# Attention and feed-forward in one Trainium2 kernel: loading, casting and turning the first five half batches by units of tokens, feed-forward chunks of 384, and a new order of work

## The chip, the cores and the metric

The kernel runs on one core of one Trainium2 chip. The metric is the device time of one execution in microseconds (us). The kernel before takes 337.58 us in the median of the four runs taken beside the changed one (337.21 to 337.86). Two kernels are compared only on fast runs of the same chip, unless the text says otherwise.

## The reference, cut to what matters

```python
# q, k, v: (batch 8, heads 8, sequence 576, head_dim 64), float32
scores = q @ k^T / 8
rel = i - j
mask  = (0 <= rel < 32)                        for heads 0..3   # plain window
mask  = (0 <= rel < 128) & (rel % 4 == 0)      for heads 4..7   # dilated window
attn  = softmax(where(mask, scores, -1e9))
x     = (attn @ v) as (4608 tokens, 512)       # heads side by side
h     = x @ w_in                               # (4608, 2048)
out   = max(0.01 h, h) @ w_out                 # (4608, 512), float32
```

## The kernel before: the parts that matter here

The work is a hand-written list of steps, and every engine does its part of the steps in the order of the list. A half batch `n` is four heads of one batch: even `n` has the plain window, odd `n` the dilated one. `lq`, `lv`, `lw` load q and k, v, and weights. `cq`, `cv`, `cw` cast them to float16 on VectorE (`V`), GpSimd (`P`) or ScalarE (`A`). `B` turns q and k on TensorE, `T` turns them by a DMA. `S`, `M`, `D` are scores, mask and values of one attention unit (three units to a half batch). `I:c:j` is a tile of the first feed-forward layer for chunk `c` of tokens, `O:t:g` a quarter of the second layer's tile `t`. `Z` is filler: matmuls on zeros whose result nobody reads.

```python
CHUNKS = [(0, 384), (384, 192), (576, 448)] + [(1024 + 512 * i, 512) for i in range(7)]
NPE = 5                     # the first five half batches are turned on TensorE

def load_qk(n, pairs=(0, 1)):
    b, kind = divmod(n, 2)
    base = (b * H + 4 * kind) * S * D
    for nm, x in (("q", q), ("k", k)):
        ...
        if n >= NPE:
            nc.sync.dma_start(t[0:96], rows_ap(x, base, [[D, 96], [96 * D, 24], [1, D]]))
        elif len(pairs) == 2:
            nc.sync.dma_start(t[:, 0:18, :].rearrange("p (a t) d -> p a (t d)", a=2),
                              rows_ap(x, base, [[9 * D, 128], [2 * S * D, 2], [1, 9 * D]]))
        else:                # one pair of heads: 128 partitions of 9 tokens
            p = pairs[0]
            nc.sync.dma_start(t[:, 9 * p:9 * p + 9, :].rearrange("p t d -> p (t d)"),
                              rows_ap(x, base + 2 * S * D * p, [[9 * D, 128], [1, 9 * D]]))
...
def pe_transpose(n, p, nm, eng):      # 9 x 2 transposes of 64 x 64 for one pair, then one copy
    ...
def values(u, log_recip=False, pool=None):
    ...
    if log_recip:                     # 1 / den on ScalarE
        nc.scalar.activation(out=ln, in_=den[:, 0:384], func=AF.Ln)
        nc.scalar.activation(out=rec, in_=ln, func=AF.Exp, scale=-1.0)
    else:                             # 1 / den on VectorE
        nc.vector.reciprocal(out=rec, in_=den[:, 0:384])
...
def ff_in(c, j):
    t0, w = CHUNKS[c]
    hp = psm.tile([128, 512], FP32, tag="pm", name="hp")
    for i in range(4):
        nc.tensor.matmul(hp[:, 0:w], w1[j // 4][:, i, j % 4::4], xT[:, i, x0:x0 + w], ...)
    nc.scalar.activation(out=gt[:, j, g0:g0 + w], in_=hp[:, 0:w], func=AF.Prelu, alpha=0.01)
```

The softmax here doesn't subtract the row's maximum and nothing guards it: scores larger than these inputs give would overflow.

## Time and profile before

| | kernel before |
|---|---|
| time | 337.58 us |
| TensorE busy | 97% |
| first feed-forward matmul | 27.40 us |
| first matmul of chunk 2 | 63.68 us |
| filler | 59 matmuls, 21.8 us |

Each digit of the page's slices is a fortieth of the span (8.4 us here), in tenths: the TensorE clock that was granted, and the mean busy share of the 16 DMA engines.

```profile
PEclk9999999999999999999999999999999999999999
DMA  6999899790499399999669945700110020011011
```

The clock row shows full speed throughout, but it can't be trusted for the first 7 us: there the fillers of a pair start 380 to 400 ns apart, and from 8.3 us on 215. The DMA engines are nearly full from the second slice on. (Shares a little above 1 occur in the views by stretch; read them as full.) The second view is the first line of the timeline of SyncE, the engine that issues the loads; its columns are start, duration, and the transfer issued.

```profile
0.80 0.41 SPq L149 DMA_DIRECT2D qf<-in_q_dram  x1
```

### The profile page before, as it was taken

To read this page: it belongs to the slowest core of one execution; us is meant where nothing else is said; L and a number is where in the kernel's file an instruction comes from. 1 tells how busy PE (TensorE), PEld (TensorE's weight loads), DVE (VectorE), ACT (ScalarE), POOL (GpSimd) and SP (SyncE) were. 2 spreads that over 40 slices of the span, in tenths; PEclk is the share of its full clock that TensorE was granted. 3 is DMA by queue.
4 is the path that set the end of the run, shared out by engine and by line. 5 is a ranking of instruction groups with operands and counts; after the bars stand their busy time and mean duration, and the time that the engine had idled before them with its cause. 6 is when DMAs were issued, how large, how long until landed. Compare 5 with 4: busy or idle time off the path is not lost.

```text
span 337.6 us, 6297 instructions
## 1 busy us (share of the span) xinstructions
PE 326.7 (97%) x2639; PEld 168.6 (50%) x2639; DVE 173.0 (51%) x190; ACT 171.3 (51%) x293; POOL 95.0 (28%) x93
## 2 busy tenths in 40 slices
PE   7999898999999899999999999999999999999995
PEld 1456576554544455445545544554455445445542
DVE  6354598631416958777786687677677200000000
ACT  2388788762434763356426743565255416524611
POOL 5446674434004335547071533300000000000000
PEclk9999999999999999999999999999999999999999
DMA  6999899790499399999669945700110020011011
GB/s 208 287 392 376 285 292 337 177 193 31 135 261 283 86 234 242 227 288 222 155 166 242 212 107 162 174 3 0 64 62 2 8 85 33 0 62 64 0 57 67
DMA packets 111243, 53.02 MB, mean 157 GB/s; under 512 B 96880, under 2 KB 101488, under 8 KB 110704
## 3 DMA queue, kind: packets, MB, share of 16 engines
q1 hardware_dynamic: 106032, 43.20, 51.5%
q10 hardware_dynamic: 5184, 9.44, 7.7%
q8 instruction: 20, 0.33, 0.4%
q14 instruction: 7, 0.06, 0.1%
HBM read 36.70 MB, written 9.44 MB: 137 GB/s over the span
## 4 chain that ended last, share of the span: by engine, by line
PE 90%; DVE 5%; issue 1%; DMA 1%; ACT 1%; DVEq 0%
PE op L353 36%; PE hp L343 34%; PE wp L396 6%; PE sps L255 6%; PE den L281 4%; PE o L289 2%; PE tp L206 2%; DVE rec L297 2%; DVE em L265 2%; DMA out_dram<-ob 1%; DVE xT L313 1%; PE sps L243 1%; ACT ln L294 0%; ACT ob L357 0%; DVE vh L189 0%
## 5 line engine op out<-in xcount | busy, mean ns | idle before, releaser
L343 PE MATMUL hp<-xT,w 128*128 128x512 f16 (+3 forms) x640 | 130.9, 359 | 0.0
L353 PE MATMUL op<-w,gt 128*128 128x512 f16 x576 | 128.8, 379 | 0.0
L345 ACT ACTIVATE gt<-hp 128x512 f16<-128x512 f32 (+3 forms) x160 | 88.0, 554 | 43.0 <-PE hp L343 42.3
L297 DVE RECIPROCAL rec<-den 128x384 f32<-128x384 f32 x32 | 81.8, 2557 | 42.5 <-PE den L281 42.5
L343 PEld LDWEIGHTS <-w 128*128 128x128 f16 x640 | 68.9, 114 | 52.8 <-issue 1.2
L353 PEld LDWEIGHTS <-gt 128*128 128x128 f16 x576 | 54.9, 98 | 64.6
L357 ACT COPY ob<-op 128x512 f32<-128x512 f32 x36 | 21.1, 587 | 82.3 <-PE op L353 82.3
L313 DVE TENSOR_TENSOR xT<-o,rec 128x192 f16<-128x192 f32 (+3 forms) x72 | 34.6, 508 | 34.1 <-ACT rec L295 30.8
L258 ACT ACTIVATE er<-sps 128x768 f16<-128x768 f32 (+1 forms) x48 | 38.8, 808 | 24.0 <-PE sps L255 21.9
L265 DVE TENSOR_TENSOR em<-er,mask 128x768 f16<-128x768 f16 (+1 forms) x42 | 30.8, 736 | 2.2 <-ACT er L258 2.2
L396 PE MATMUL wp<-xT 128*128 128x512 f16 x59 | 21.8, 420 | 3.2 <-DVE xT L112 1.3
L189 POOL CAST vh<-vf 128x2048 f16<-128x2048 f32 (+1 forms) x8 | 13.5, 1682 | 39.5 <-PE o L289 21.6
L176 POOL CAST qh<-qf 96x768 f16<-96x768 f32 x16 | 14.3, 921 | 36.2 <-DMA qf<-in_q_dram 35.9
L255 PEld LDWEIGHTS <-kT 64*128 64x128 f16 (+1 forms) x448 | 14.8, 121 | 17.0 <-issue 16.1
L255 PE MATMUL sps<-qT,kT 64*128 64x96 f16 (+1 forms) x448 | 22.9, 229 | 0.0
L176 POOL CAST kh<-kf 96x768 f16<-96x768 f32 x20 | 17.6, 904 | 5.0 <-DMA kf<-in_k_dram 4.3
L289 PEld LDWEIGHTS <-vh 128*64 128x64 f16 (+1 forms) x448 | 15.8, 110 | 3.4 <-DVE xT L313 0.7
L281 PE MATMUL den<-em,ones 128*64 128x384 f16 (+1 forms) x84 | 14.8, 349 | 2.4 <-DVE em L265 2.2
L185 POOL CAST vh<-vf 128x1536 f16<-128x1536 f32 x6 | 9.0, 1503 | 28.1 <-PE o L289 22.8
L330 POOL CAST w<-wf 128x2048 f16<-128x2048 f32 x7 | 13.9, 1983 | 7.4 <-DMA wf<-in_moe_w_out_dram 4.3
L289 PE MATMUL o<-em,vh 128*64 128x96 f16 (+1 forms) x392 | 14.8, 201 | 0.6 <-DVE xT L313 0.6
L281 PEld LDWEIGHTS <-ones 128*64 128x64 f16 (+1 forms) x96 | 5.7, 106 | 11.0 <-issue 6.7
(52 smaller groups left out, 115.4 us busy)
## 6 DMA issues: line engine op xcount, KB each, us to landing
out_dram<-ob ACTq DMA_DIRECT2D x36, 256.0 KB, 2.1
qf<-in_q_dram SPq DMA_DIRECT2D x14, 576.0 KB, 5.5
kf<-in_k_dram SPq DMA_DIRECT2D x14, 576.0 KB, 7.0
wf<-in_moe_w_in_dram SPq DMA_DIRECT2D x4, 1024.0 KB, 11.1
wf<-in_moe_w_out_dram SPq DMA_DIRECT2D x4, 1024.0 KB, 9.0
vf<-in_v_dram SPq DMA_DIRECT2D x7, 576.0 KB, 6.6
vf<-in_v_dram SPq DMA_DIRECT2D x7, 384.0 KB, 6.8
vf<-in_v_dram SPq DMA_DIRECT2D x9, 192.0 KB, 4.5
```

The costliest lines, as they stand in the source:

```text
L176: eng(out=t[0:96, 12 * D * p:12 * D * p + 12 * D].rearrange("p (t h d) -> p h t d", t=6, h=2), in_=f[0:96, 12 * p:12 * p + 12, :].rearrang ...
L255: nc.tensor.matmul(sps[0:kp, hh, w * x:w * x + w], ka, qa, start=not pe_mask, stop=not pe_mask or x == len(tiles) - 1)
L258: nc.scalar.activation(out=er[0:kp], in_=sps[0:kp, :, 0:384], func=AF.Exp, scale=SCALE)
L265: nc.vector.tensor_tensor(out=em[0:kp].rearrange("p h (t c) -> p h t c", c=w), in0=er[0:kp].rearrange("p h (t c) -> p h t c", c=w), in1=ba ...
L281: nc.tensor.matmul(den[64 * hh:64 * hh + 64, 0:384], ones[0:kp], em[0:kp, hh, :], start=True, stop=True)
L289: nc.tensor.matmul(o[64 * hh:64 * hh + 64, w * x:w * x + w], vt[0:kp, sl, :], em[0:kp, hh, w * x:w * x + w], start=True, stop=True)
L297: nc.vector.reciprocal(out=rec, in_=den[:, 0:384])
L313: nc.vector.tensor_tensor(out=out_x, in0=ins[0], in1=ins[1], op=ALU.mult)
L343: nc.tensor.matmul(hp[:, 0:w], w1[j // 4][:, i, j % 4::4], xT[:, i, x0:x0 + w], start=(i == 0), stop=(i == 3))
L345: nc.scalar.activation(out=gt[:, j, g0:g0 + w], in_=hp[:, 0:w], func=AF.Prelu, alpha=0.01)
L353: nc.tensor.matmul(op, gt[:, j, g0:g0 + 128], w2[g][:, j % 4, :], start=(j == 0), stop=(j == 15))
L396: nc.tensor.matmul(wp, warm[:, 0:128], warm, start=True, stop=True)
```

## The change

The intent was to start the feed-forward layers earlier. In the first five half batches, loads, casts and transposes follow attention units: 384 tokens of one pair of heads (units 0 and 1), or 192 tokens of both pairs (unit 2), so that scores can begin as soon as the first unit has landed. Chunks of 384 tokens follow the same units. The list is rewritten, with the second layer between tiles of the first, less filler, and more reciprocals as a logarithm and an exponential on ScalarE. The core of the diff:

```diff
-CHUNKS = [(0, 384), (384, 192), (576, 448)] + [(1024 + 512 * i, 512) for i in range(7)]
-RING = 2048
-GRING = 1024
+CHUNKS = [(0, 384), (384, 192), (576, 384), (960, 192)] + [(1152 + 384 * i, 384) for i in range(9)]
+RING = 2304
+GRING = 1152
@@ PROGRAM: all of it replaced; its start
-Z:2 Z:2 mask Z:1 lq:1:0 Z:2 Z:1 Z:1 lq:0:0 cq:0:q:V:0 Z:2 lv:1:0 Z:1 lq:1:1 Z:1 lq:0:1 cq:0:k:A:0
+Z:5 lq:1:1 lq:0:0 lq:1:0 cq:1:q:V:1 Z:2 cq:0:q:A:0 cq:0:k:V:0 lq:0:1 lq:0:2 lv:1:A Z:6 cq:1:k:A:1
... (cut)
@@ load_qk, the first five half batches
-            elif len(pairs) == 2:
-                nc.sync.dma_start(t[:, 0:18, :].rearrange("p (a t) d -> p a (t d)", a=2),
-                                  rows_ap(x, base, [[9 * D, 128], [2 * S * D, 2], [1, 9 * D]]))
             else:
-                p = pairs[0]
-                nc.sync.dma_start(t[:, 9 * p:9 * p + 9, :].rearrange("p t d -> p (t d)"),
-                                  rows_ap(x, base + 2 * S * D * p, [[9 * D, 128], [1, 9 * D]]))
+                w = 3 if us == "2" else 6
+                for p in (0, 1) if us == "2" else UNITS[us]:
+                    c0, t0 = (12 + 3 * p, 384) if us == "2" else (6 * p, 0)
+                    nc.sync.dma_start(t[:, c0:c0 + w, :].rearrange("p t d -> p (t d)"),
+                                      rows_ap(x, base + (2 * S * p + t0) * D, [[S * D, 2], [w * D, 64], [1, w * D]]))
... (load_v, cast_qk, cast_v and pe_transpose by units in the same way: cut)
-            for lo, hi in ((0, cut), (cut, length)):     # results split where the ring of 2048 wraps
+            out_x = xT[:, 2 * kind + (s if s < 2 else x), pos:pos + length]
```

## The prediction

> **What bounds the kernel now.** I read the page's busy line first, then the groups by shape, then one line's busy time by stretch of the span, then the timeline of TensorE.
>
> ```profile
> PE 326.7 (97%) x2639; PEld 168.6 (50%) x2639; DVE 173.0 (51%) x190; ACT 171.3 (51%) x293; POOL 95.0 (28%) x93
> ```
> TensorE is the bound, and no other engine is above 51%. But 97% is not 97% useful. The groups of TensorE by shape:
>
> ```profile
> L353 PE MATMUL op<-w,gt 128*128 128x512 f16 x576 | 128.8, 379 | 0.0
> L343 PE MATMUL hp<-xT,w 128*128 128x512 f16 x448 | 101.1, 380 | 0.0
> L396 PE MATMUL wp<-xT 128*128 128x512 f16 x59 | 21.8, 420 | 3.2 <-DVE xT L112 1.3 <-ACT ln L294 0.3
> L343 PE MATMUL hp<-xT,w 128*128 128x384 f16 x64 | 11.3, 327 | 0.0
> L343 PE MATMUL hp<-xT,w 128*128 128x192 f16 x64 | 6.2, 248 | 0.0
> ```
> wp is filler: 59 matmuls whose result nobody reads, 21.8 us. They stand where TensorE would otherwise wait. Where they lie (the busy time of that line in five stretches; columns: stretch, length, TensorE busy and count, weight loads, clock, DMA share, GB/s):
>
> ```profile
> 0.00:27.40 27.40, 16.52 (x45) 3.90 (x45) 1.00 0.93 304
> 27.40:63.70 36.30, 5.19 (x15) 1.03 (x14) 1.00 0.96 300
> 63.70:125.00 61.30, 0.14 (x1) 0.00 (x0) 1.00 0.72 173
> ```
> The timeline of TensorE at the two ends of the bad part:
>
> ```profile
> 26.31 1.25 PE L396 MATMUL wp<-xT 128*128 128x512 f16 x3
> 27.40 2.11 PE L343 MATMUL hp<-xT,w 128*128 128x384 f16 x12
> ```
> ```profile
> 62.37 1.47 PE L396 MATMUL wp<-xT 128*128 128x512 f16 x4
> 63.68 0.54 PE L343 MATMUL hp<-xT,w 128*128 128x448 f16 x2
> ```
> The first feed-forward matmul starts at 27.40, chunk 2 at 63.68. Only chunks 0 and 1 (576 tokens, some 16 us of TensorE) lie between, as the second layer isn't begun before 76.
>
> From the start-to-start times I made a ledger of the span: filler 21.8, stalls that no filler covers 5.9 (3.7 of them between 27.4 and 63.7, 1.8 near 115, 0.5 near 259), first start 1.33, last start to the end 337.62 - 333.64 = 4.0. The rest is useful: 304.6 us. After 63.7 the loss is 2.3 us in 270. So **all that a new order can win lies before 63.7**: 16.6 of filler before 27.4, 5.2 of filler and 3.7 of stall after it.
>
> **What the Trainium skill says.** (1) "Trainium Kernel Development and Optimization", Performance Expectations: matmul busy time is a bad metric. The trace agrees: 97% holds 21.8 us of filler. (2) "TensorE: Matmul & The Clock Gate", Part 1: warm start-to-start is N/2.4 ns plus about 2.5 ns, cold N/1.2. The trace: 59 matmuls of 512 columns between 279.69 and 292.42 are 215.8 ns each; the first fillers stand 427 ns apart within a group up to about 7 us. So 384 columns should cost (384/2.4 + 2.5) 162.5 ns; chunk 0 shows 163, 166 with its share of switches. (3) "ScalarE: Activation LUTs": 0.833 ns an element plus a fixed part. The groups here:
>
> ```profile
> L345 ACT ACTIVATE gt<-hp 128x512 f16<-128x512 f32 x112 | 66.8, 597 | 35.6 <-PE hp L343 34.9
> L345 ACT ACTIVATE gt<-hp 128x384 f16<-128x384 f32 x16 | 7.7, 490 | 2.4 <-PE hp L343 2.4
> L295 ACT ACTIVATE rec<-ln 128x384 f32<-128x384 f32 x16 | 8.4, 523 | 0.5
> L294 ACT ACTIVATE ln<-den 128x384 f32<-128x384 f32 x16 | 7.8, 488 | 2.8 <-PE den L281 2.8
> L297 DVE RECIPROCAL rec<-den 128x384 f32<-128x384 f32 x32 | 81.8, 2557 | 42.5 <-PE den L281 42.5
> ```
> (597 - 490)/128 = 0.836 ns an element: it agrees. (4) "DMA: Bandwidth & Descriptors", Specifications: line rate needs 512 B and up. The stretch 24 to 30 (2,048 and 2,304 B packets) against 46 to 48 (256 B), last column GB/s:
>
> ```profile
> 24.00:30.00 6.00, 5.89 (x87) 3.61 (x89) 3.20 (x6) 5.30 (x11) 3.03 (x4) 1.00 1.04 404
> 46.00:48.00 2.00, 2.00 (x28) 1.74 (x25) 1.87 (x1) 1.69 (x5) 1.35 (x1) 1.00 1.19 254
> ```
> It agrees.
>
> **The change part by part.**
>
> *Useful TensorE work.* The first layer goes from 640 to 832 matmuls: 704 of 384 and 128 of 192 columns. By the chunks' own means (stalls out): 704 x 0.166 + 128 x 0.087 = 128.0 against 127.3 before: +0.7. One mask by matmul less: -0.4. Transposes stay at 360. Entries from feed-forward into attention work, about 0.1 us each, go from 44 to 40 by the order of TensorE: -0.4. Switches between the layers rise from 15 to 127, but the one at 109 shows no cost. Sum: 304.6 - 0.1 = 304.5.
>
> *Filler.* 59 become 27, all before the first feed-forward matmul.
>
> *When the first feed-forward matmul starts (T0).* It needs units 0, 1, 3, 4 of attention. Packet records before 60 us average 18.7 ns for 256 B, 53 for 1,024, 88.5 for 2,048; I read 71 for 1,536 and 42 for 768 between them. Over 16 engines batch 0 is q and k 7.2 us, v 1.9 + 2.7: with the first bytes at 2.0 and 1 us to land, the last v lands near 15. Hand chain, by durations of before scaled to the new sizes: VectorE's clearing ends at 6.3 and its first cast at 6.6; 15 fillers, mostly cold, take TensorE to 8.0; first transposes 8.0, first scores 9.7, then ScalarE's row of copies, casts and exponentials (6 exp x 0.81, 5 ln and rec x 1.01, 5 casts and some 7 copies x 0.5) brings the scores of units 3, 0, 1, 2 to 12.3, 14.5, 16.1, 17.9. v of the even heads is cast on VectorE behind the product of unit 4 (1.8 + 1.3 us: 17.9 to 20.9), so unit 0 gets its values at 21.0; ln and rec of units 0 and 1 one after the other end at 23.6, the last product at 24.4. **T0 = 24.0**, 3.4 earlier than before. The first group of w_in (2.8 us of DMA after v) is cast by 20.5; the later ones by 25, 27 and 29 against needs at 26.6, 29 and 32.
>
> *After T0.* Useful work before T0 is 6 scores, 5 values, 6 transposes: 9.6. What follows is 304.5 - 9.6 = 294.9, plus 4.0 of end. The gap before chunk 2 is filled: between T0 and chunk 2 stand 32 steps of the first layer and now 15 steps of the second (four matmuls of 512 columns each, 15 x 4 x 0.218 = 13 us), with 6 scores, 5 values and 6 transposes. That puts chunk 2 near T0 + 38 = 62. Bytes up to v of batch 1 (16 MB) land near 51 at the rates above, so in time.
>
> *Stalls left.* VectorE is relieved: reciprocals 32 to 11, -21 x 2.56 = -54 us. ScalarE gets them: +21 x 1.01 = 21, +9 for narrower activations (704/4 x 0.49 + 32 x 0.33 = 97 against 88), and more casts: some 215 us, 66%. The second layer's accumulators now stay open while first-layer tiles run: one open in 116 of 208, two in 29, three in 5, of four PSUM buffers. From the banks given at the build I counted where TensorE comes back to a bank sooner than its reader can be done: the larger places are 0.65 us (after the values of unit 47) and 0.46 (after unit 26), in all some 2.5 us. With ScalarE's queueing and a late transfer or so I choose **4.0** (before: 11.1 of stall and filler after T0).
>
> Sum: 24.0 + 294.9 + 4.0 + 4.0 = 326.9, say **327.0 us**, -3.2%.
>
> **Rivals.** *A: ScalarE takes the place.* For: it has 66% over the whole and its queue is in order; the 192-column chunk asks for one activation of 0.33 us every 0.33 us, with copies and exponentials between; few filler or spare buffers remain to hide a late one. Against: 512-column stretches left it 43 us idle on the same line. It would leave 8 to 10 us of stall: 332. *B: the start is hidden by the loads anyway.* DMA share is 0.93 to 0.96 up to 63.7, so work ordered earlier may just wait for bytes; smaller packets cost q and k of batch 0 7.2 instead of 6.9 us of the engines (1,024 of 107 ns over 16). T0 would be 26.5 and the second layer would wait for w_out: 332 to 334. *C: a cold TensorE.* With fewer fillers, the early part runs at half rate: up to 3.4 us of half rate, +1.7. *D: the order was fitted better than my hand chain*: T0 at 21.5 and stalls of 2: 322.
>
> **Range and chances.** T0 is good to about 2 us, stalls to about 3, together 3.6; 80% would be 327 -5/+6, with a longer tail upwards for A and B: 321 to 334. Faster by over 2% means under 330.9, one such deviation above the middle: 0.80. Same 0.18, slower 0.02.
>
> **What would show it.** Right: filler near 10 us (27 matmuls), first hp matmul at 22 to 26, chunk 2 near 62 with op matmuls before it from about 43, TensorE's stalls after T0 within 2 to 7 us, reciprocals x11, ScalarE busy 210 to 220, mean start-to-start of hp at 384 columns 163 to 168 ns. Wrong if hp starts after 26 (B), if TensorE's waits name ScalarE's gt or er at over 5 us (A), if the 384-column matmuls keep over 175 ns, or if the end stretches beyond 4 us after the last matmul.

## More of the kernel before

A single run of a kernel on one core has no known state, and it is called so where it occurs.

An access pattern is a list of [step, count], the slowest dimension first. The source of a pair's load is `[[9 * D, 128], [1, 9 * D]]`: 128 rows of 9 tokens (2,304 B).

A load of one pair, 288 KB (2 heads x 576 tokens x 64 x 4 B), keeps the queue for 0.41 us.

## The result, and the profile after

The changed kernel takes **423.60 us** (median of four runs, 422.44 to 424.21), against 337.58 of the kernel before. The ratio is 1.2545, with a 95% interval of 1.2514 to 1.2576. A ratio here is the mean time of one kernel's fast runs over the mean of the other's in the same rounds, so it is not quite the ratio of the medians. The prediction was 327.0 us, so even its sign was wrong.

The page of the profiled run (span 420.7 us) has these lines: busy time, the slices (10.5 us each now), and the shares of the chain that ended last.

```profile
PE 332.9 (79%) x2797; PEld 193.8 (46%) x2797; DVE 131.9 (31%) x197; ACT 204.2 (49%) x401; POOL 53.8 (13%) x64
...
PEclk9555559856587777999999999999999999999999
DMA  0112393143814147986999959999282100000111
...
PE 59%; SPq 21%; DMA 15%; DVE 3%; POOL 1%; issue 1%; ACT 1%; ACTq 0%; DVEq 0%
```

TensorE fell from 97% to 79% busy. The clock is at half in most of the first twelve slices. The most telling row is the last of the slices: the DMA engines stood at 0 to 2 tenths in the first four, where they had been at 6 to 9. And the queue of SyncE ("SPq"), which is in no chain of the kernel before, carries 21% of the chain. What was to be a start without waits for bytes is one that waits for bytes while the DMA engines idle.

The start and the middle by stretches (columns: stretch, length, busy and count of TensorE, weight loads, VectorE, ScalarE, GpSimd, then granted clock, DMA share, GB/s):

```profile
0.00:20.00 20.00, 8.32 (x63) 3.18 (x65) 6.01 (x16) 2.69 (x4) 3.88 (x14) 0.81 0.11 42
20.00:40.00 20.00, 6.00 (x64) 2.63 (x62) 1.43 (x4) 3.69 (x8) 0.50 (x1) 0.50 0.14 50
40.00:62.20 22.20, 13.51 (x174) 7.45 (x172) 7.56 (x15) 8.71 (x17) 2.92 (x3) 0.50 0.62 197
62.20:158.80 96.60, 47.26 (x461) 29.86 (x459) 19.29 (x32) 31.41 (x67) 8.89 (x8) 0.73 0.38 124
158.80:260.00 101.20, 101.03 (x931) 62.04 (x931) 46.38 (x63) 70.88 (x140) 28.36 (x29) 0.98 0.88 193
```

Up to 40 us even TensorE, the busiest engine, works only 14.3 us, a good part of it filler, and 42 to 50 GB/s move. The DMA share of 0.14 is close to two engines of sixteen, which would be 0.125. After 158.8 TensorE is busy 101.03 of 101.20 us. So the whole loss lies before 158.8. The timeline of SyncE shows how:

```profile
0.80 0.71 SPq L157 DMA_DIRECT2D qf<-in_q_dram  x1
1.57 0.52 SPq L157 DMA_DIRECT2D kf<-in_k_dram  x1
2.13 2.22 SPq L157 DMA_DIRECT2D qf<-in_q_dram  x1
4.40 3.83 SPq L157 DMA_DIRECT2D kf<-in_k_dram  x1
8.27 3.82 SPq L157 DMA_DIRECT2D qf<-in_q_dram  x1
```

The fourth to the eighth load, of 192 KB each (2 x 384 x 64 x 4 B), hold the queue for 3.82 us each, nine times as long as one of 288 KB before. 192 KB in 3.82 us is 51 GB/s, which is the whole rate of the stretch 20 to 40. TensorE waits some 8 us at a time for what lies behind these loads. One such wait, then T0 and the start of chunk 2, in TensorE's timeline (in brackets: idle time before, and what ended it):

```profile
16.38 0.53 PE L209 MATMUL tp<-ident,kh 64*64 64x64 f16 x12 [8.04 <-ACT kh L179]
...
62.25 1.44 PE L339 MATMUL hp<-xT,w 128*128 128x384 f16 x4
...
146.55 2.11 PE L339 MATMUL hp<-xT,w 128*128 128x384 f16 x12
158.85 1.44 PE L339 MATMUL hp<-xT,w 128*128 128x384 f16 x4 [10.18 <-ACT gt L341]
```

The first feed-forward matmul starts at 62.25 us (I call this time T0, as the prediction does) instead of 27.40, and chunk 2 at 146.55 instead of 63.68. The wait at 158.85 is named after ScalarE; but ScalarE itself stood in its queue behind a cast of k that waited for bytes. From start-to-start times I counted TensorE's stalls that no filler covers: 32.7 us before T0, 53.0 from there to 158.8, and 0.5 in all the rest.

### The profile page after: what moved, and what is told of

Its sections match the earlier page's. It is cut to its first block, busy times and chain, and to the rows that moved or that the text cites. A ratio compares the mean times of both kernels' runs of the same rounds, so it can differ in the third digit from the quotient of the medians.

```text
span 420.7 us, 6734 instructions
## 1 busy us (share of the span) xinstructions
PE 332.9 (79%) x2797; PEld 193.8 (46%) x2797; DVE 131.9 (31%) x197; ACT 204.2 (49%) x401; POOL 53.8 (13%) x64
## 4 chain that ended last, share of the span: by engine, by line
PE 59%; SPq 21%; DMA 15%; DVE 3%; POOL 1%; issue 1%; ACT 1%; ACTq 0%; DVEq 0%
PE op L349 26%; PE hp L339 26%; SPq L157 19%; DMA wf<-in_moe_w_in_dram 4%; DMA kf<-in_k_dram 4%; DMA wf<-in_moe_w_out_dram 4%; PE sps L260 3%; DMA qf<-in_q_dram 3%; PE den L286 2%; DVE rec L300 2%; PE o L292 1%; SPq L164 1%; SPq L168 1%; POOL w L326 1%; DVE xT L309 0%
## 5 line engine op out<-in xcount | busy, mean ns | idle before, releaser
L339 PE MATMUL hp<-xT,w 128*128 128x384 f16 (+1 forms) x832 | 144.9, 322 | 23.6 <-DVE qT L213 13.2
L349 PE MATMUL op<-w,gt 128*128 128x512 f16 x576 | 140.8, 385 | 0.0
L341 ACT ACTIVATE gt<-hp 128x384 f16<-128x384 f32 (+1 forms) x208 | 94.0, 466 | 81.0 <-PE hp L339 77.8
L339 PEld LDWEIGHTS <-w 128*128 128x128 f16 x832 | 91.9, 116 | 69.9 <-issue 28.0
L309 DVE TENSOR_TENSOR xT<-o,rec 128x384 f16<-128x384 f32 (+1 forms) x64 | 33.9, 553 | 81.9 <-ACT rec L298 76.7
L300 DVE RECIPROCAL rec<-den 128x384 f32<-128x384 f32 x11 | 28.1, 2555 | 20.9 <-PE den L286 20.9
L353 ACT COPY ob<-op 128x512 f32<-128x512 f32 x36 | 21.0, 584 | 28.0 <-PE op L349 27.4
L209 PE MATMUL tp<-ident,kh 64*64 64x64 f16 x180 | 7.0, 224 | 33.2 <-POOL kh L179 23.7
L297 ACT ACTIVATE ln<-den 128x384 f32<-128x384 f32 x37 | 18.0, 486 | 8.3 <-PE den L286 8.3
L189 DVE CAST vh<-vf 128x1536 f16<-128x1536 f32 (+2 forms) x12 | 12.7, 1057 | 24.3 <-DMA vf<-in_v_dram 24.3
L298 ACT ACTIVATE rec<-ln 128x384 f32<-128x384 f32 x37 | 19.4, 525 | 1.2
```

The costliest lines, as they stand in the source:

```text
L209: nc.tensor.transpose(tp[r, 64 * t:64 * t + 64], h[r, t, :], ident[r, r])
L309: nc.vector.tensor_tensor(out=out_x, in0=ins[0], in1=ins[1], op=ALU.mult)
L349: nc.tensor.matmul(op, gt[:, j, g0:g0 + 128], w2[g][:, j % 4, :], start=(j == 0), stop=(j == 15))
L353: nc.scalar.copy(out=ob, in_=op)
```

## The experiments

**Theory T**: the pattern `[[S * D, 2], [w * D, 64], [1, w * D]]` has two heads as its slowest dimension, and a transfer is dealt out to the DMA engines along that dimension, so only 2 of 16 engines work for it. **Rival Q**: the loads became too many (40 instead of 14 for these half batches) or their packets too small, whatever the engines. **Rival O**: the order of work or the chunks of 384 are bad in themselves. In the expectations T is called theory E, Q is rival S, and `hp` stands for the matmuls of the first feed-forward layer; the letters in experiments 7 and 8 mean what is said there.

All kernels below passed the comparison with the reference.

### 1. Each unit load as two transfers of one head

The pattern's slowest dimension becomes 64. 80 transfers take the place of 40.

```diff
-                    nc.sync.dma_start(t[:, c0:c0 + w, :].rearrange("p t d -> p (t d)"),
-                                      rows_ap(x, base + (2 * S * p + t0) * D, [[S * D, 2], [w * D, 64], [1, w * D]]))
+                    for hh in range(2):
+                        nc.sync.dma_start(t[64 * hh:64 * hh + 64, c0:c0 + w, :].rearrange("p t d -> p (t d)"),
+                                          rows_ap(x, base + (S * (2 * p + hh) + t0) * D, [[w * D, 64], [1, w * D]]))
```

> The changed kernel with one edit: each q/k unit of two heads is loaded by two transfers of 64 partitions, one for a head, instead of one whose source pattern is [2 heads][64 rows][row]. Bytes and packet sizes stay, the order of work stays. Theory E (the pattern with a slowest dimension of 2 puts each of these loads on 2 of the 16 DMA engines): the DMA share in the first 60 us rises from 0.13 to above 0.6, the first hp matmul moves from 62 to 23-28 us, and the time falls to 327 (322 to 334), the number I had predicted. Rival S (the loads are small, 96 to 192 KB in 768 and 1,536 B packets, and that is what makes them slow): the time stays above 390, as these loads become smaller still. Rival O (the new order and the chunks of 384 cost by themselves): above 345 with the DMA share high.

Measured: 350.00 us (348.08 to 350.68), ratio to before 1.0328 (1.0278 to 1.0378). T0 came down from 62.25 to 34.23. Doubling the number of transfers took 74 us away: rival Q alone cannot do that, and T has its direction. But 327 was expected, so something is left; the time is also above the 345 that rival O had named, though O asked for full DMA engines with it. The DMA share of the first 60 us rose to 0.66, but in the first 20 us it is only 0.41, and SyncE issues one transfer every 0.64 us. With 96 KB to a transfer, that pace allows about 154 GB/s (98,304 B in 0.64 us, an estimate).

### 2. Both pairs of a head in one transfer, where both are asked for

```diff
+                ps = (0, 1) if us == "2" else UNITS[us]
+                c0, t0 = (12, 384) if us == "2" else (6 * ps[0], 0)
+                for hh in range(2):
+                    nc.sync.dma_start(
+                        t[64 * hh:64 * hh + 64, c0:c0 + w * len(ps), :].rearrange("p (a t) d -> p a (t d)", t=w),
+                        rows_ap(x, base + (S * (2 * ps[0] + hh) + t0) * D,
+                                [[w * D, 64], [2 * S * D, len(ps)], [1, w * D]]))
```

> The changed kernel with its q/k loads by one transfer for a head and both head pairs where both are asked for: 16 engines, 48 transfers for q and k of the first five half batches instead of the 80 of the run with heads apart. Theory E: within 1% of the run with heads apart. If the number of transfers (0.45 us of the queue's time for each) bounds the start, it is 2 to 8 us faster than that run.

Measured: 336.77 us (336.17 to 337.53), ratio 0.9951 (0.9918 to 0.9984): the same as before. That is 13.2 us faster than experiment 1, more than the 2 to 8 expected. With 48 transfers T0 is 28.51. The first loads in SyncE's timeline, then the stretch 8 to 16 us:

```profile
0.80 1.23 SPq L158 DMA_DIRECT2D qf<-in_q_dram  x2
```
```profile
8.00:16.00 8.00, 5.61 (x111) 3.08 (x110) 2.07 (x5) 4.71 (x9) 0.50 (x1) 1.00 0.52 144
```

Two transfers in 1.23 us replace one of 0.41 us for more bytes. So DMA is at 0.52 where the kernel before has 1.02. What is left of Q is real, though small beside T: a load on 64 partitions costs some 0.6 us of the queue, and units need many.

### 3. Repair for batch 0 alone

The loads of half batches 0 and 1 as in experiment 1, those of 2 to 4 left as changed.

```diff
+                    if n < 2:
+                        for hh in range(2):
+                            nc.sync.dma_start(...as in experiment 1...)
+                        continue
```

> The changed kernel where only batch 0 (half batches 0 and 1) gets its q and k on 16 engines; half batches 2 to 4 keep the pattern with slowest dimension 2. Theory E: the first hp matmul at 23-28 us, then the 30 remaining two-engine loads (3.5 MB at some 50 GB/s: 71 us) hold up batch 1, so stalls lie between 35 and 110 us, and the time is 365 to 385. Rival O: the start stays late, above 45 us.

Measured: 396.63 us, in one run (state unknown). T0 is 34.03, as late as in experiment 1 and not at 23 to 28 as expected, and the stalls come back after it (time from one matmul's start to the next one's): 9.4 us at 46.9, 8.3 at 56.5, 14.4 at 70.7, and so on to 131. That is 12 us above the range expected, so I had put the share of the later loads too low. The direction stands: the late half batches' loads cost more than half of the loss (about 47 of the 74 us that experiment 1 won).

### 4. The same pattern put into the kernel before: 2, 4 and 8 engines

Only the eight q and k loads of batch 0 are changed. Their rows are taken in another order, so that the slowest dimension is 2, 4 or 8; bytes, packets, transfers and order of work stay.

```diff
-                                  rows_ap(x, base + 2 * S * D * p, [[9 * D, 128], [1, 9 * D]]))
+                                  rows_ap(x, base + 2 * S * D * p, [[9 * D, 2], [9 * D * 2, 64], [1, 9 * D]]))
```

(The others have 4, 32 and 8, 16; the three are b2, b4 and b8.) The tokens of q and k in batch 0 are thus permuted. The outputs still passed the comparison, as q and k are 0.1 times a normal draw and the softmax is nearly flat; that is no sign that the loads are right.

> The kernel before with one edit: the eight q/k loads of batch 0 (288 KB each, 2,304 B packets, same bytes and same number of packets) read their rows in the order [2][64], so that the slowest dimension is 2. The output is wrong on purpose (rows are permuted). Theory E: each of these loads takes some 128 x 107 ns / 2 = 6.9 us on two engines, 55 us in all instead of 7, the first hp matmul moves from 27.4 to 65-75 us and the time to 370-385 us. Rival S: packets of 2,304 B stay fast, within 2% of 337.6. Rival O: nothing of the new order is in it, within 2% of 337.6.

> As b2 with the slowest dimension 4. Theory E (the slowest dimension's length, where it is under 16, is the number of engines): each of the eight loads takes some 128 x 107 ns / 4 = 3.4 us, 27 us in all; the first hp matmul at 40-46 us, the time 350 to 358.

> As b2 with the slowest dimension 8: 1.7 us a load, 14 us in all; the first hp matmul at 30-34 us, the time 339 to 345. If only a slowest dimension of 2 were a special case: 337.6 within 1%, for 4 and for 8.

| slowest dimension | T0, us | time, us |
|---|---|---|
| 128 (kernel before) | 27.40 | 337.58 |
| 8 | 30.34 | 340.67 |
| 4 | 42.98 | 355.09 |
| 2 | 64.03 | 377.18 |

All three are single runs (state unknown). With 4 and 2 the steps are far above a run's scatter; with 8 the time is not: in the rounds of that run the kernel before took 337.59 to 339.52, so only T0, 2.9 us later, carries that row. Part of its delay may be the queue's: each of these loads held SyncE for at least 0.60 us with 8, against 0.41 to 0.43 before. SyncE's timeline with 2:

```profile
2.14 3.94 SPq L149 DMA_DIRECT2D qf<-in_q_dram  x1
6.12 5.60 SPq L149 DMA_DIRECT2D kf<-in_k_dram  x1
```

288 KB in 5.60 us is 53 GB/s, as in the changed kernel (51), and from 20 to 35 us the DMA share is 0.13, two engines of sixteen. All values lie in the ranges expected, but for T0 with 2, which is 1 us below its range. This is the decisive experiment: the slowest dimension by itself, with the number of transfers and the order untouched, makes the wait, and in the dose that T says. Q and O cannot explain it. (The rows are also read in another order here; but the changed kernel reads its rows in their own order, and its loads are as slow.)

### 5. Loads, casts and transposes by pairs again, new order and chunks kept

```diff
-                w = 3 if us == "2" else 6
-                for p in (0, 1) if us == "2" else UNITS[us]:
-                    c0, t0 = (12 + 3 * p, 384) if us == "2" else (6 * p, 0)
-                    nc.sync.dma_start(t[:, c0:c0 + w, :].rearrange("p t d -> p (t d)"),
-                                      rows_ap(x, base + (2 * S * p + t0) * D, [[S * D, 2], [w * D, 64], [1, w * D]]))
+                if us == "2":
+                    continue
+                ps = UNITS[us]
+                nc.sync.dma_start(
+                    t[:, 9 * ps[0]:9 * ps[-1] + 9, :].rearrange("p (a t) d -> p a (t d)", t=9),
+                    rows_ap(x, base + 2 * S * D * ps[0], [[9 * D, 128], [2 * S * D, len(ps)], [1, 9 * D]]))
```

(The casts and the transposes take 9 columns of a pair likewise; steps for unit 2 do nothing.)

> Undoes one part of the change: q and k of the first five half batches are loaded, cast and turned by head pairs with all 576 tokens (rows of 9 tokens, 2,304 B, one transfer of 128 partitions on 16 engines) as in the kernel before; the order of work and the chunks of 384 stay. Theory E with the rate of issues (0.64 us of the queue for each of the many transfers bounded the first 18 us of the run with pairs together): the queue issues 8 transfers for q and k of batch 0 instead of 24, batch 0 has landed by 16 us instead of 22.5, the first hp matmul is at 24-26.5 instead of 28.5, stalls after it fall below 8 us, and the time is 327 to 332. Rival U (the units are what lets the new order start early): the first hp matmul later than 28 us and the time above 337.

Measured: 329.53 us (328.48 to 331.85), ratio 0.9726 (0.9684 to 0.9768). On another chip, beside experiment 7 and the second run of experiment 6:

> The run with pair loads once more, for comparison on the same chip: 329.5 within 0.5%.

There: 329.86 us (328.79 to 333.41), ratio 0.9757 (0.9688 to 0.9826). T0 is 25.89 and 25.55. So rival O falls: what is left of the change is worth about 2.5%, inside the range that had been predicted for the whole (321 to 334 us). What the change did not need was its first item, the units: on 16 engines they give 336.77 (experiment 2), without them 329.53. Units loaded in one cheap transfer over 16 engines were not tried.

### 6. Loads of k of batch 0 from ScalarE's queue

Once with units (experiment 2 as the base), once with pairs (experiment 5 as the base).

```diff
-                    nc.sync.dma_start(
+                    (nc.scalar if nm == "k" and n < 2 else nc.sync).dma_start(
```

> The run with pairs together, its k loads of batch 0 issued from ScalarE's queue instead of SyncE's. Theory (rate of issues bounds the first 18 us): q/k of batch 0 have landed at some 14 instead of 19.6 us, the first hp matmul at 24.5 to 26.5 instead of 28.5, the time 331 to 334. Rival (the engines are the limit, or ScalarE's own 0.6 us for each issue delays its casts as much): no change within 1 us, or slower.

Measured with units: 330.90 us (330.26 to 331.70), ratio 0.9778 (0.9742 to 0.9813). The time is a little below what was expected, but not for the reason given: T0 is 29.34, no earlier than in experiment 2, as the rival had said. ScalarE's timeline says why:

```profile
7.17 4.32 ACTq L158 DMA_DIRECT2D kf<-in_k_dram  x4
11.53 0.51 ACT L182 CAST kh<-kf 128x384 f16<-128x384 f32 x1 [4.19 <-DMA qf<-in_q_dram]
```

Four issues hold ScalarE from 7.17 on, and the cast of k behind them starts only at 11.53, while TensorE waits for it. What was won came later: stalls after T0 fell from 7.3 to 0.7 us.

> The run with pair loads, with the four k loads of batch 0 issued from ScalarE's queue. SyncE then issues v by 3 us instead of 5. The DMA share of the first 8 us is 0.73, so there is at most 2 us to win: the loads land 0.5 to 1.5 us earlier, and under theory L the time falls by 0.5 to 1.5 us; if the engines' rate alone counts, it stays within 0.5 us.

Measured with pairs: 328.79 us (328.04 to 332.28, five runs), ratio 0.9695 (0.9645 to 0.9745), beside 329.86 of the same kernel on one queue. The intervals overlap, and the profiled run, the slowest of the five (332.28), has T0 at 26.15: inconclusive.

### 7. v cast before the product of unit 4

The prediction's hand chain had the cast of v of half batch 0 behind the product of unit 4 on VectorE, "17.9 to 20.9". It can go ahead: one step of experiment 5's list is moved.

```diff
-... lq:3:2 S:0:b D:4:lp cv:0:V:b Z:1 S:1:b ...
+... lq:3:2 S:0:b cv:0:V:b D:4:lp Z:1 S:1:b ...
```

> The run with pair loads, with VectorE's cast of the v of half batch 0 put ahead of the product of unit 4. In the run with pair loads VectorE sits idle from 14.7 to 16.6 us with that v landed at 14.5, and unit 0 waits for the cast until 20.9. Theory T (the time follows the first hp matmul): it moves from 25.9 to 23-24 us and the time falls by 2 to 3 us, to 326.5-327.5. Theory L (after the first hp matmul the loads bind; the DMA share is above 1 from 8 to 48 us): the first hp matmul moves as much, but chunk 2 still starts at 66.5-67.5 us and the time falls by under 1 us.

Measured: **323.24 us** (322.71 to 323.87), ratio 0.9544 (0.9501 to 0.9587). T0 is 21.45, and chunk 2 starts at 60.02 instead of 65.00 in the second run of experiment 5, so theory L falls. This version beats both kernels. It is 6.6 us faster than experiment 5 on the same chip (the medians), more than twice what was expected. TensorE's timeline around T0 in experiment 5 (its second run), then in experiment 7:

```profile
20.63 0.53 PE L289 MATMUL o<-er,vh 128*64 128x96 f16 x7 [2.30 <-DVE vh L196]
...
25.55 4.70 PE L336 MATMUL hp<-xT,w 128*128 128x384 f16 x26
```
```profile
21.45 2.79 PE L336 MATMUL hp<-xT,w 128*128 128x384 f16 x16
```

Three things changed at once. The first is the wait itself: the cast starts some 2 us earlier. The timelines of VectorE and GpSimd show the second. Experiment 5:

```profile
17.09 0.96 DVE L192 CAST vh<-vf 128x1536 f16<-128x1536 f32 x1
18.08 2.49 DVE L196 CAST vh<-vf 32x1472 f16<-32x1472 f32 x1
...
17.56 2.24 POOL L323 CAST w<-wf 128x2048 f16<-128x2048 f32 x1 [8.17 <-DMA wf<-in_moe_w_in_dram]
```

Experiment 7:

```profile
15.04 0.96 DVE L192 CAST vh<-vf 128x1536 f16<-128x1536 f32 x1 [0.47 <-DMA vf<-in_v_dram]
16.04 0.92 DVE L196 CAST vh<-vf 32x1472 f16<-32x1472 f32 x1
...
17.79 1.89 POOL L323 CAST w<-wf 128x2048 f16<-128x2048 f32 x1 [8.09 <-DMA wf<-in_moe_w_in_dram]
```

The second cast of v takes 2.49 us where it overlaps GpSimd's cast of weights (17.56 to 19.80) and 0.92 where it does not. From 19.80 to its end at 20.57 are 0.77 us: it did nearly all of its work after GpSimd was done. The Trainium skill's "SBUF — State Buffer", section "SBUF: two separate sides", says that the port pair shared by VectorE and GpSimd is an exclusive lock: of a GpSimd instruction and a VectorE instruction that needs the pair, the one that starts first holds it for its whole length, and the other waits. This trace agrees (0.77 us after GpSimd's end, of the 0.92 that the cast takes alone). In the first run of experiment 5 it was the other cast, 2.65 us instead of 0.96. The move takes both casts out of that collision.

The third is the clock (stretch 16 to 24 us of the second run of experiment 5, then of experiment 7):

```profile
16.00:24.00 8.00, 5.25 (x68) 3.08 (x65) 6.86 (x7) 5.25 (x10) 4.32 (x3) 0.71 1.05 390
```
```profile
16.00:24.00 8.00, 7.38 (x96) 4.86 (x95) 4.16 (x7) 7.54 (x15) 1.89 (x1) 1.00 1.01 305
```

In experiment 5 TensorE waited 2.30 us for the values' v, and was at half clock from 19.4 to 26.2; in experiment 7 it was not. No run separates how much of the 6.6 us each of the three is worth.

### 8. Filler over that wait

Experiment 5 with ten filler matmuls (`Z:10`) ahead of `D:0:lp`, to keep the clock up without moving the cast.

> The run with pair loads with ten more filler matmuls (10 x 0.22 = 2.2 us) just ahead of the values of unit 0, where TensorE waits 2.5 to 4 us for VectorE's cast of v and its granted clock falls to 0.74 between 16 and 24 us. Theory C (the wait lets TensorE fall to half its clock, and the first 10 or so hp matmuls and the matmuls before them pay for it): the first hp matmul moves from 25.6-25.9 to 24.5-25.5 us, no hp matmul of the first chunk starts 320 ns after another (all at 163), and the time falls by 1 to 3 us, to 327-329. Rival: the filler only takes the place of the wait, and the time stays within 0.5 us of 329.7, or rises.

Measured: 328.93 us (327.83 to 330.11), ratio 0.9702 (0.9621 to 0.9783), on a third chip. The profile has the clock at 1.00 from 8 to 32 us and T0 at 24.19, 1.4 to 1.7 us earlier than the two runs of experiment 5, and no first-layer matmul of the first chunk starts 320 ns after another. So with the wait covered the clock stayed up, and T0 came earlier. In the time, 0.6 to 0.9 us against experiment 5's medians is within the scatter and across chips: inconclusive. The profiled run lost part again to a wait of 2.05 us for a cast of v, without half clock after it (nine matmuls of 512 columns in 2.12 us):

```profile
47.72 0.53 PE L257 MATMUL sps<-qT,kT 64*128 64x96 f16 x8 [2.05 <-DVE vh L192]
48.18 2.12 PE L346 MATMUL op<-w,gt 128*128 128x512 f16 x9
```

## Why the prediction was wrong, point by point

**The step that failed** is the sentence "Over 16 engines batch 0 is q and k 7.2 us", in the sum for T0. It took packet durations from the kernel before and divided by 16, without asking over how many engines the new pattern is dealt out. In its place, the sixteen loads of q and k of batch 0 held SyncE until 46.5 us, and the DMA share stood at 0.11 to 0.14 up to 40 us. With two engines, the forty loads (5 half batches x 2 x 590 KB = 5.9 MB) need about 115 us at 51 GB/s, an estimate from the 3.82 us of one. Experiment 4 shows the cause by itself, experiments 1, 2 and 5 show it undone. I could have read it: the Trainium skill's "DMA: Bandwidth & Descriptors", section "Why a DMA increments its semaphore by 16 and not by 1", says that the number of engines is the largest up to 16 that divides the slowest dimension (not of size 1) of both patterns, and the table "Rules for kernel authors" warns of an outermost dimension below 16. The prediction had cited another section of this page, on packet sizes, and looked at those alone. The runs agree with the page: 2, 4, 8 and 128 give T0 of 64.0, 43.0, 30.3 and 27.4.

**T0**: 24.0 predicted, 62.25 measured, +38. **Chunk 2**: 62 predicted, 146.55 measured, since the same loads feed batch 1 and half batch 4; the stalls after T0 were 53.5 us, against 4.0 predicted. With them the prediction's own sum is 62.25 + 294.9 + 4.0 + 53.5 = 414.7; the 6.0 to the span of 420.7 I put down to work at half clock in that part (0.73 granted between 62 and 159), without a run to separate it.

**Rival B** (the start hidden by the loads anyway) named the right resource, but from a DMA share of 0.95 before, with T0 at 26.5: it was mis-sized by 36 us, by the same division by 16. It expected full engines, and they were idle. **Rival C** (a cold TensorE) was real too: the clock was 0.50 from 20 to 62 us. In experiment 5 half clock lasted 6.8 us about T0, and T0 came 1.4 to 1.7 us later than in experiment 8; C had said 1.7 of time, but in the time only 0.6 to 0.9 shows, within the scatter. **Rival A** did not occur: ScalarE was 204.2 us busy (predicted 210 to 220), and after 158.8 all stalls together are 0.5 us.

**What was right.** The sum holds for three repaired kernels, with their own T0 and stalls put in: experiment 2, 28.5 + 294.9 + 4.0 + 7.3 = 334.7 for a span of 334.9; experiment 6 with units, 29.3 + 294.9 + 4.0 + 0.7 = 328.9 for 328.4; experiment 7, 21.45 + 294.9 + 4.0 + 2.4 = 322.75 for 322.1. So the useful work after T0 and the end were sized right. Experiment 7 has almost the numbers of rival D (T0 at 21.5, stalls of 2, 322 us), but with other loads and a moved cast. The groups of the changed kernel confirm the reciprocals (11 of them, 28.1 us). First-layer matmuls of 384 columns start 163 to 168 ns apart where nothing stalls them (predicted so; the groups give a matmul's own duration, which overlaps the next one: 331 ns here, 327 in the kernel before). One reading of the prediction is not in its trace: the first fillers of the kernel before start 380 to 400 ns apart within a pair, not 427, which only the later runs show; it changes nothing in the sum. The hand chain came out nearly right in experiment 5: v's casts, predicted at 17.9 to 20.9, ended at 20.91 in the first run of experiment 5, and with a warm clock T0 was 24.19 (experiment 8), for the 24.0 predicted. Part of that is luck: these runs load by pairs, and the chain was worked out for units. With units on 16 engines T0 was 28.51 (experiment 2), as the chain had nothing for the issues that such loads take there. And it took the collision of the two casts as v's price and did not see that one step could be moved, which is worth 6.6 us (experiment 7).

## What to carry to other kernels

Before any estimate that divides bytes by 16, look at the first dimension of both patterns of every new transfer: here 2, 4 and 8 left engines idle, and 64 and 128 did not. A low DMA share (0.11 to 0.14) beside engines that wait for data was the sign of it. Count the issues of finer loads: two transfers of 64 partitions at 0.6 us each took the place of one at 0.41 us, and even with the issues on two queues units (330.90) were no faster than pairs on one (329.53). Where a cast on VectorE stands behind a product that waits, or beside a cast on GpSimd, try it earlier: the wait, the port and the clock may all be saved at once.

## What the Trainium skill lacked or had wrong

- "DMA: Bandwidth & Descriptors": the number of engines is right as stated, as said above. It does not say what happens to the issuing queue: with two engines at work, later issues held SyncE for 3.82 us (192 KB) or 5.60 us (288 KB), so transfers behind it that would use all 16 engines wait too (the first issue of v took 5.57 us in experiment 4 with 2 engines, and 0.43 in the kernel before).
- The same page does not say how the cost of an issue depends on the transfer's shape. Here a load of a pair on 128 partitions held the queue for 0.41 to 0.43 us, and a load on 64 partitions mostly for 0.57 to 0.61. The number of partitions is not the whole of it: the same 288 KB on 128 partitions with a slowest dimension of 8 held it for 0.60 to 0.65 (experiment 4, after the first). Why, no run here tells.
- "DMA: Bandwidth & Descriptors", section "Issuing engines are not separate DMA queues", says that a second issuing engine saves only issue time. It does not say that the issuing engine's own work waits behind its issues: four of them held ScalarE's casts for 4.32 us in experiment 6.
- "TensorE: Matmul & The Clock Gate", Part 1, speaks of an idle window of about 3.4 us. Here half clock began during a wait of TensorE of 2.30 us (experiment 5), so a shorter wait is no assurance; a wait of 2.05 us in experiment 8 brought none. What decides between the two no run here tells.
